# The rational feed-forward after a channel attention: the second product's input as two float32r parts, numerator and denominator as completed squares, in one arm of a branch

## The chip, the cores and the metric

One core of a Trainium2 chip. The metric is the device time of one execution in microseconds (us), the median of the runs; a smaller number is better. The engines are named as the profile names them: PE (TensorE, matrix products), ACT (ScalarE), DVE (VectorE), POOL (GpSimd) and SP (the queue that issues the DMAs here). SBUF is the on-chip memory, PSUM the banks that PE writes to.

## What is computed

```python
qn = q / (norm(q, axis=1) + 1e-6);  kn = k / (norm(k, axis=1) + 1e-6)   # q, k, v: 4 x 6080 x 256
s  = kn.transpose(0, 2, 1) @ qn / tau                                  # 256 x 256 per batch
a  = softmax(s)
x  = (v @ a).reshape(24320, 256)
h  = x @ w_in                                                          # 24320 x 2048
P  = a0 + a1*h + a2*h**2 + a3*h**3
Q  = 1 + |b0|*|h| + |b1|*h**2
out = (P / (Q + 1e-6)) @ w_out                                         # 24320 x 256
```

`w_in` and `w_out` are float64, all else is float32. The coefficients that the reference draws by default are a = (0.505, -0.235, -0.287, 0.280) and b = (-3.213, 3.898).

## The kernel before

The attention matrix is folded into the weights of the first layer: for each batch the kernel sums k'q over 24 half blocks of rows (`Attn.half`), makes the softmax (`Attn.softmax`) and multiplies it into `w_in` (`fuse`), which gives for each of 8 blocks of 256 hidden columns a high and a low float32r part (`whi`, `wlo`). After that the work is a long stream of pairs. There are 48 groups of tokens (12 per batch: 11 of 512 tokens and one of 448), and each group runs through 8 pairs (`pair`, line 620), a pair being 2 x 128 hidden columns by 512 tokens, 1024 elements on each of 128 partitions. So there are 384 pairs, worth 380 of full width.

A pair before has these steps (lines 633 to 696):

- `mm1` on PE: 12 float32r products (high x high, high x low, low x high) of 512 columns into `hx`, one of three PSUM slots.
- The denominator in `d`, in one of two forms. Five of eight pairs take the plain form: ACT squares `hx`, POOL makes b1*h^2 + 1 (`line`), ACT makes |b0*h| in `kk`, POOL adds the two (`sum`). The pairs in `FACTORED` (three of eight) take ACT, then DVE (`prod`), then ACT again.
- The numerator: ACT makes a3*h + a2 in `y`, DVE multiplies by h (`num1`), adds a1 and multiplies by h again (`num2`).
- The reciprocal: ACT takes the reciprocal root of `d` and squares it (`r`), POOL multiplies d*r (`again`; with `one` before it on factored pairs), DVE adds a0 and multiplies by r (`quot`), and DVE multiplies by 2 - d*r (`last`), a correction step, into `g`.
- `mm2` on PE: 4 float32 products of `g` with `w_out_sb`, each of which appears in the trace as two instructions of 512 columns, summed over the 8 pairs in `acc` (PSUM).

`values` loads v, transposes it on DVE and splits it in two (`vhi` on ACT, `vlo` on POOL) once per group, and `finish` transposes `acc` on DVE and stores it. While a batch runs, the next batch's 24 half blocks are squared on ACT, summed up on POOL (`ssq`) and multiplied on PE into an `hx` slot, which DVE adds to `sacc`.

At the start `piece` turns the float64 weights into float32 by integer steps on DVE (12 of the 16 pieces before the first pairs, in `EARLY`), beside the first batch's attention.

What sets the order: `Planner.order` (line 133) goes through all steps with a list of costs (the second argument of `step`) and priorities (`LAG`, `TIME`), picks for each engine the ready step of the lowest key whose buffers are free, and writes out one fixed order for each engine. `keep_in_program_order` holds each engine to it. A step marked `port`, and any step on POOL, isn't started by the planner beside another such step on the other of the two engines DVE and POOL.

Of the kernel before, what the change touches and what calls it, by code (L numbers as in the profile page):

```python
# [10 lines left out]
F32 = mybir.dt.float32  # L11
U32 = mybir.dt.uint32
F32R = mybir.dt.float32r
AF = mybir.ActivationFunctionType
# [6 lines left out]
LAG = {  # L21
    "first": (0.84, 4.52, 2.78, 3.73, 4.53, 2.33, 3.41, 3.6),
    "prod": (-11.23, -0.03, -11.23, 6.14, -11.23, -11.23, 5.27, -11.23),
    "abs": (-35.28, -33.04, -35.28, -60.18, -35.28, -35.28, -12.39, -35.28),
    "line": (-60.83, 30.85, 1.23, -9.96, -64.93, -61.3, 25.68, -3.97),
    "second": (3.47, 5.1, 5.85, 6.25, 8.47, 6.18, 3.15, 4.97),
    "sum": (-75.1, -80.53, -59.16, -66.42, -83.56, -73.41, -47.34, -36.63),
    "slope": (6.9, 4.95, 7, 7.41, 9.07, 6.95, 6.12, 6.22),
    "num1": (80.21, 21.96, 120.89, 23.72, 98.59, 65.28, 53.4, 94.99),
    "num2": (91.21, 77.02, 48.39, 83.69, 132.26, 79.9, 92.26, 66.3),  # L30
    "root": (-17.03, -9.24, -6.87, -5.73, -6.19, -9.62, -12.27, -14.71),
    "one": (18.62, -22.45, 18.62, 2.61, 18.62, 18.62, 25.53, 18.62),
    "square": (-78.86, -34.07, -129.08, -42.44, -147.95, -117.98, -7.49, -107.82),
    "again": (-10.9, -52.88, -8.31, -23.6, -7.9, 6.38, -36.31, -6.49),
    "quot": (38.4, 26.11, 35.76, 10.27, 43.7, 29.95, 4.71, 41.91),
    "last": (-3.36, 0.17, -3.01, -4.4, 0.77, 1.56, -1.89, -4.37),
    "out": (24.58, 54.15, 41.53, 45.99, 18.94, 61.33, 13.35, 15.28),
    "in": (-5.72, -5.59, -3.14, -6.52, -2.09, -4.66, -7.12, -10.04), "in_n": 0,
}
TIME = {  # L40
    "pair": 3.576, "start": 61.026, "load": 1.674, "softmax": 52.628, "in": 4.243, "late_in": 1.499,
    "out0": 30.295, "out": 5.035, "attn0_0": -1.487, "attn_0": 1.155, "attn0": 4.026, "attn": 1.97,
    "attn1": 91.474, "value": 54.159, "fuse": 1.698, "finish": 21.052, "front": 41.363,
    "front_pace": 1.762, "ahead": 15.518, "vhi": 26.968, "vlo": 25.086,
# [38 lines left out]
class Planner:  # L83
# [17 lines left out]
    def add(self, eng, cost, key, fn, reads=(), writes=(), port=False):  # L101
# [20 lines left out]
        for b in {id(b): b for b in (*reads, *writes)}.values():  # L122
            if b.tag is not None:
                b.left += 1
                s.bufs.append(b)
# [7 lines left out]
    def order(self):  # L133
# [19 lines left out]
        def fits(s):  # L153
            want = {}
            for b in s.new:
                want[b.tag] = want.get(b.tag, 0) + 1
                if b.tag in queue and queue[b.tag][-1] is not s:
                    return False
            if any(b.owner != s.eng and b.until > now for b in s.banks):
                return False  # L160
            return all(len(free[t]) >= n for t, n in want.items())
# [55 lines left out]
def tile_channel_attention_rational_ffn(  # L217
# [25 lines left out]
    while n0 < N:  # L243
# [7 lines left out]

    FACTORED = (1, 3, 6)

    EARLY = [("in", m) for m in range(8)] + [("out", m) for m in range(4)]

    FRONT = 12

# [6 lines left out]
    SLOTS = {"hx": 3, "acc": 1, "d": 4, "uu": 4, "r": 3, "g": 4, "w": 10, "kq": 4, "sq": 2, "ssq": 1,  # L264
             "vst": 1, "vhi": 2, "vlo": 2, "orow": 2, "sacc": 1, "eT": 1, "cv": 1, "cv2": 1, "n2": 1,
             "s0": 1, "y": 1, "e": 1, "sm": 1}
    plan = Planner(SLOTS, ("d", "uu", "r", "g", "w", "kq", "sq", "cv", "cv2", "vst", "vhi", "vlo", "orow", "acc"), ("hx", "acc"))

# [3 lines left out]

    homes = {}

    def buf(tag, shape, dtype=F32, name=None):


        def view(slot):
            sizes = dict(zip("abc", shape[1:]))
            t = homes[tag][slot]  # L280
            if t.dtype != dtype:
                t = t.bitcast(dtype)
            t = t[:, : math.prod(shape[1:])]
            names = " ".join(sizes)
            return t.rearrange(f"p ({names}) -> p {names}", **sizes) if len(sizes) > 1 else t

        homes.setdefault(tag, 0)
        homes[tag] = max(homes[tag], math.prod(shape[1:]))
        return Buf(tag, view)

    def step(eng, cost, key, fn, reads=(), writes=(), port=False):
        new = [b for b in writes if b.tag is not None and not b.writers]

        def run():
            for b in new:
                b.tile = b.view(b.slot)
            fn()

        plan.add(eng, cost, key, run, reads, writes, port)
# [6 lines left out]
    coef = const.tile([P, 7], F32, name="coef")  # L306
    sp.dma_start(coef[:, 0:4], ca.partition_broadcast(P))
    sp.dma_start(coef[:, 4:6], cb.partition_broadcast(P))
    sp.dma_start(coef[:, 6:7], tau.partition_broadcast(P))
    a0, a1, a2, a3 = (coef[:, i : i + 1] for i in range(4))  # L310
    rtau = const.tile([P, 1], F32, name="rtau")
    dve.reciprocal(rtau, coef[:, 6:7])

    babs = const.tile([P, 2], F32, name="babs")
    act.activation(babs, coef[:, 4:6], AF.Abs)
    b0, b1 = babs[:, 0:1], babs[:, 1:2]
# [458 lines left out]
```

## Time and profile before

| | |
|---|---|
| median of 3 runs | 2646.99 us (2646.87 to 2647.03) |
| span of the profiled execution (first to last instruction) | 2645.5 us |
| PE busy | 2595.5 us, 98% |
| DVE, POOL, ACT busy | 2259.8, 2216.3, 2124.2 us |
| chain that ended last | PE 88% |
| granted TensorE clock, mean | 0.995 of full speed |

The page gives no time of the profiled execution beside its span; the median of the other runs lies 1.5 us above it. "Busy" of PE is modelled from the starts of pipelined matmuls, so the chain and the distance between starts are read, not the mean of one instruction. In the timelines the start of one instruction is often ahead of the end of the one before on the same engine; what one costs in a full stream is the distance from its start to the next start.

### The profile page before, as it was taken

The numbers are of one execution on the slowest core, as the hardware profiler recorded it, in microseconds if no ns is written. First come the engines' busy times: TensorE is split into PE (matmuls) and PEld (weight loads), VectorE is DVE, ScalarE is ACT, GpSimd is POOL, SyncE is SP. The second block draws the span as 40 slices with busy tenths as digits, with TensorE's granted clock in tenths as the row PEclk, the third lists the DMA queues.
The fourth block names the chain that finished last, engine by engine and source line by source line (L and its number), as shares of the span: only waits on it lengthen the run. The fifth ranks groups of instructions, "written<-read, shape, count | busy, mean of one in ns | idle before, by whom it ended". The sixth has DMA issues, their size and how long they took to land.

```text
span 2645.5 us, 26474 instructions
## 1 busy us (share of the span) xinstructions
PE 2595.5 (98%) x8744; PEld 1651.8 (62%) x8744; DVE 2259.8 (85%) x2035; ACT 2124.2 (80%) x2179; POOL 2216.3 (84%) x1152
## 2 busy tenths in 40 slices
PE   7899999999999999999999999999999999999998
PEld 6656666666666666666666666665666566666665
DVE  6898888988978787888888878888897889889887
ACT  5688888888878778788878778778887888888886
POOL 6889888888778999788878899878885888888886
PEclk9899999999999999999999999999999999999999
DMA  9512311111112222211121222211111111111101
GB/s 306 153 25 64 68 19 25 23 17 24 17 35 53 48 65 53 48 24 17 23 40 16 49 68 51 46 25 17 23 25 17 18 22 24 22 18 25 23 9 15
DMA packets 457017, 109.76 MB, mean 41 GB/s; under 512 B 405168, under 2 KB 453808, under 8 KB 456880
## 3 DMA queue, kind: packets, MB, share of 16 engines
q1 hardware_dynamic: 456880, 108.07, 19.4%
q8 instruction: 69, 1.13, 0.2%
q14 instruction: 68, 0.56, 0.1%
HBM read 83.10 MB, written 24.90 MB: 41 GB/s over the span
## 4 chain that ended last, share of the span: by engine, by line
PE 88%; ACT 4%; DVE 3%; DMA 2%; issue 1%; POOL 1%; SPq 0%; DVEq 0%; ACTq 0%; POOLq 0%
PE acc L58 45%; PE hx L58 43%; ACT uu L58 1%; DVE hx L58 1%; DMA r<-in_k_dram 1%; ACT r L58 1%; ACT d L58 1%; POOL d L58 0%; DVE uu L58 0%; DMA r<-in_q_dram 0%; DMA kq<-in_k_dram 0%; SPq L58 0%; ACT sq L58 0%; DVE g L58 0%; POOL ssq L58 0%
## 5 line engine op out<-in xcount | busy, mean ns | idle before, releaser
L58 PE MATMUL acc<-g,w_out_sb 128*128 128x512 f32 (+1 forms) x3072 | 1349.7, 588 | 4.5 <-DVE orow L58 4.4
L58 POOL TENSOR_TENSOR d<-d,r 128x1024 f32<-128x1024 f32 (+1 forms) x384 | 906.5, 2364 | 166.9 <-ACT r L58 155.0
L58 PE MATMUL hx<-vhi,w 128*128 128x512 f32 (+1 forms) x3072 | 961.4, 420 | 7.4 <-DVE g L58 5.3
L58 PEld LDWEIGHTS acc<-g,w_out_sb 128*128 128x128 f32 x3072 | 581.2, 189 | 618.6 <-issue 592.4
L58 PEld LDWEIGHTS hx<-vhi,w 128*128 128x128 f32 x3072 | 578.2, 189 | 229.4 <-issue 94.3
L58 POOL TENSOR_TENSOR d<-d,uu 128x1024 f32<-128x1024 f32 (+1 forms) x243 | 575.6, 2369 | 35.0 <-ACT uu L58 20.5
L58 DVE TENSOR_TENSOR uu<-uu,hx 128x1024 f32<-128x1024 f32 (+1 forms) x384 | 462.4, 1204 | 149.9 <-ACT uu L58 148.8
L58 DVE SCALAR_TENSOR_TENSOR hx<-hx,coef,r 128x1024 f32<-128x1024 f32 (+1 forms) x384 | 489.2, 1275 | 111.3 <-ACT r L58 106.9
L58 ACT ACTIVATE d<-hx 128x1024 f32<-128x1024 f32 (+1 forms) x243 | 247.1, 1017 | 345.7 <-PE hx L58 338.6
L58 DVE SCALAR_TENSOR_TENSOR hx<-uu,coef,hx 128x1024 f32<-128x1024 f32 (+1 forms) x384 | 487.7, 1273 | 4.2
L58 DVE SCALAR_TENSOR_TENSOR g<-d,hx 128x1024 f32<-128x1024 f32 (+1 forms) x384 | 461.0, 1201 | 21.6 <-POOL d L58 15.0
L58 PE MATMUL hx<-vlo,w 128*128 128x512 f32 (+1 forms) x1536 | 473.7, 390 | 0.0
L58 ACT ACTIVATE uu<-hx,babs 128x1024 f32<-128x1024 f32 (+1 forms) x384 | 425.9, 1109 | 50.7 <-PE hx L58 50.7
L58 ACT ACTIVATE uu<-hx,coef 128x1024 f32<-128x1024 f32 (+1 forms) x384 | 461.4, 1201 | 1.3 <-DVE d L58 1.3
L58 ACT ACTIVATE r<-d 128x1024 f32<-128x1024 f32 (+1 forms) x384 | 405.4, 1056 | 20.2 <-POOL d L58 17.8
L58 ACT ACTIVATE r<-r 128x1024 f32<-128x1024 f32 (+1 forms) x384 | 405.2, 1055 | 6.8
L58 POOL TENSOR_SCALAR d<-d,babs 128x1024 f32<-128x1024 f32 (+1 forms) x243 | 272.2, 1120 | 133.8 <-ACT d L58 130.7
L58 PEld LDWEIGHTS hx<-vlo,w 128*128 128x128 f32 x1536 | 288.9, 188 | 60.7
L58 DVE SCALAR_TENSOR_TENSOR d<-uu,babs,hx 128x1024 f32<-128x1024 f32 (+1 forms) x141 | 178.2, 1264 | 33.7 <-ACT uu L58 33.4
L58 POOL TENSOR_SCALAR d<-d,ones 128x1024 f32<-128x1024 f32 (+1 forms) x141 | 157.5, 1117 | 36.7 <-ACT r L58 36.6
L58 POOL TENSOR_TENSOR ssq<-sq,ssq 128x1024 f32<-128x1024 f32 (+1 forms) x69 | 166.0, 2406 | 24.0 <-ACT sq L58 19.5
L58 ACT ACTIVATE d<-d 128x1024 f32<-128x1024 f32 (+1 forms) x141 | 146.8, 1041 | 9.8 <-DVE d L58 9.8
(82 smaller groups left out, 1119.1 us busy)
## 6 DMA issues: line engine op xcount, KB each, us to landing
vst<-in_v_dram SPq DMA_DIRECT2D x352, 64.0 KB, 2.3
out_dram<-orow SPq DMA_DIRECT2D x352, 64.0 KB, 2.0
kq<-in_k_dram SPq DMA_DIRECT2D x78, 256.0 KB, 3.8
kq<-in_q_dram SPq DMA_DIRECT2D x78, 256.0 KB, 4.2
d<-in_moe_w_in_dram SPq DMA_DIRECT2D x8, 512.0 KB, 7.0
r<-in_k_dram SPq DMA_DIRECT2D x10, 256.0 KB, 6.5
r<-in_q_dram SPq DMA_DIRECT2D x10, 256.0 KB, 6.5
d<-in_moe_w_out_dram SPq DMA_DIRECT2D x4, 512.0 KB, 8.2
```

The costliest lines, as they stand in the source:

```text
L58: ins = op(*args, **kwargs)
```

## The change

Steps of a pair, in the arm that runs when the tests on the coefficients hold:

- The hidden layer is scaled (by `grow`, put into the softmax's reciprocal) and the constants are transformed, so that the denominator is 1 + (|h| + centre)^2 and the numerator (h * ((reach*h + shift)^2 + drop) + a0'). ACT makes |h| and the square in `d`, the square in `y`; DVE makes `num` from `y` and `hx`. The plain and factored forms, `kk` and `num1` are gone in this arm.
- ACT makes the reciprocal root of d + 1 and squares it (`r`), as before.
- DVE makes gh = (num + a0') * r, rounded to float32r (`high`), then (d + 1) * gh (`back`, both inputs in SBUF, marked `port`), then num + a0' minus that (`rest`); POOL multiplies this remainder by r into gl (`low`, float32r).
- `w_out` is split in `piece` into `w_high` and `w_low` (float32r). `mm2` is 8 float32r products of gh with both, and 4 of gl with `w_high`.
- The test on the coefficients (4|a1||a3| >= a2^2, 3.5|b1| >= b0^2, and bounds) is computed on DVE at the start, loaded into a register of every engine, and a branch chooses between two complete programs, each with its own planned order. The loads of the first 7 half blocks stand ahead of the branch. The constants of the arm are made in `squares()` behind it.
- Slots: `uu` 3 (was 4), `w` and `w2` 9 (10), `orow` 1 (2), `g` becomes `gh` 3 and `gl` 2. The tables `LAG` and `TIME` are new, and so all the orders; `FACTORED` goes.

With the coefficients above, 4|a1||a3| = 0.264 against a2^2 = 0.082, and 3.5|b1| = 13.6 against b0^2 = 10.3.

```diff
 def pair(m, at, vparts, w, acc):
...
-        if m >= NFP and p in FACTORED:
...
-            step("POOL", 2.36 * s, at + LAG["sum"][p], fn, [d, kk], [d])
-        fn = lambda: act.activation(c(y), c(hx), AF.Identity, scale=a3, bias=a2)
-        fn = lambda: dve.tensor_tensor(c(y), c(y), c(hx), op=ALU.mult)
-        fn = lambda: dve.scalar_tensor_tensor(c(hx), c(y), a1, c(hx), op0=ALU.add, op1=ALU.mult)
+            if fast:
+                    on("ACT", 0.94, "size", lambda: act.activation(c(d), c(hx), AF.Abs), [hx], [d])
+                on("ACT", 1.06, "bow", lambda: act.activation(c(d), c(d), AF.Square, bias=centre), [d], [d])
+                fn = lambda: act.activation(c(y), c(hx), AF.Square, scale=reach, bias=shift)
+                on("ACT", 1.09, "slope", fn, [hx], [y])
+                fn = lambda: dve.scalar_tensor_tensor(c(hx), c(y), drop, c(hx), op0=ALU.add, op1=ALU.mult)
+                on("DVE", 1.2, "num", fn, [y, hx], [hx])
...
-        fn = lambda: pool.tensor_tensor(c(d), c(d), c(r), op=ALU.mult)
-        fn = lambda: dve.scalar_tensor_tensor(c(hx), c(hx), a0, c(r), op0=ALU.add, op1=ALU.mult)
-        fn = lambda: dve.scalar_tensor_tensor(
-            c(g), c(d), 2.0, c(hx), op0=ALU.subtract, op1=ALU.mult, reverse0=True
-        )
+            fn = lambda: dve.scalar_tensor_tensor(c(out), c(hx), base_a0, c(r), op0=ALU.add, op1=ALU.mult)
+            on("DVE", 1.2, "high", fn, [hx, r], [out])
...
+                fn = lambda: dve.scalar_tensor_tensor(c(d), c(d), 1.0, by(), op0=ALU.add, op1=ALU.mult)
+                on("DVE", 1.2, "back", fn, [d, near], [d], True)
...
+                fn = lambda: dve.scalar_tensor_tensor(c(into), c(hx), base_a0, c(d), op0=ALU.add, op1=ALU.subtract)
+                on("DVE", 1.2, "rest", fn, [hx, d], [into])
...
+                    on("POOL", 2.36, "low", lambda: pool.tensor_tensor(c(gl), c(d), c(r), op=ALU.mult), [d, r], [gl])
+                parts = ((1.82, "out_hi", gh, (w_high, w_low)), (0.91, "out_lo", gl, (w_high,)))
...
+    halves = {fast: arm(fast) for fast in (True, False)}
+    choice = nc.values_load(plain[0:1, 0:1], min_val=0, max_val=1)
+    with tc.If(choice > 0) as which:
+        squares()
+        for s in halves[True]:
+            s.fn()
+    with which.Else():
+        unscaled()
+        for s in halves[False]:
+            s.fn()
```

DVE in the middle of the stream, before. hx_90 to hx_92 are the three PSUM slots; uu<-uu,hx is `num1`, hx<-uu,coef,hx `num2`, hx<-hx,coef,r `quot`, d<-uu,babs,hx `prod`, and g is written by `last`:

```order
L58 SCALAR_TENSOR_TENSOR d_83<-uu_86,babs,hx_92 128x1024
L58 SCALAR_TENSOR_TENSOR hx_91<-uu_85,coef,hx_91 128x1024
L58 SCALAR_TENSOR_TENSOR hx_90<-hx_90,coef,r_108 128x1024
L58 SCALAR_TENSOR_TENSOR hx_91<-hx_91,coef,r_109 128x1024
L58 SCALAR_TENSOR_TENSOR g_96<-d_81,hx_90 128x1024
L58 TENSOR_TENSOR uu_87<-uu_87,hx_92 128x1024
```

Every one of these instructions has an operand in PSUM (hx).

DVE in the middle of the stream, now, in the arm that the coefficients choose. hx_68 to hx_70 are the PSUM slots, `fit` holds the constants; gh is written by `high`, hx<-uu,fit,hx is `num`, d<-d,gh `back`, d<-hx,fit,d `rest`:

```order
L56 SCALAR_TENSOR_TENSOR gh_82<-hx_70,fit,r_81 128x1024
L56 SCALAR_TENSOR_TENSOR hx_69<-uu_76,fit,hx_69 128x1024
L56 SCALAR_TENSOR_TENSOR d_75<-d_75,gh_82 128x1024
L56 SCALAR_TENSOR_TENSOR d_75<-hx_70,fit,d_75 128x1024
L56 SCALAR_TENSOR_TENSOR gh_83<-hx_69,fit,r_79 128x1024
L56 SCALAR_TENSOR_TENSOR hx_68<-uu_77,fit,hx_68 128x1024
L56 SCALAR_TENSOR_TENSOR d_73<-d_73,gh_83 128x1024
```

Four instructions make a pair; `back` has both inputs in SBUF, and `high` and `num` of later pairs stand between the `rest` of one pair and the `back` of the next. POOL's `low` becomes ready at `rest`.

PE where the first batch's fusing (hx<-w_in_sb) meets the first pair (hx<-vhi,w), before; acc<-kq is a half block of the next batch's scores:

```order
L58 MATMUL hx_92<-ident,sq_105 128x128 x4
L58 MATMUL hx_90<-w_in_sb,eT_115 128x256 x4
L58 MATMUL hx_91<-w_in_sb,eT_115 128x256 x4
L58 MATMUL hx_92<-w_in_sb,eT_115 128x256 x4
L58 MATMUL acc_89<-kq_102 128x256 x4
L58 MATMUL hx_90<-vhi_137,w_116 128x512 x2
```

Three of the eight blocks are fused ahead of the first pair, the others between the pairs that follow.

PE at the same place now (sq_100 holds the turned softmax, w_87 a part of the first fused block):

```order
L56 MATMUL hx_69<-kq_97 128x256 x4
L56 MATMUL hx_69<-kq_98 128x256 x4
L56 MATMUL hx_70<-ident,sq_101 128x128 x4
L56 MATMUL hx_68<-w_in_sb,sq_100 128x256 x4
L56 MATMUL hx_69<-w_in_sb,sq_100 128x256 x4
L56 MATMUL hx_70<-w_in_sb,sq_100 128x256 x4
L56 MATMUL hx_68<-w_in_sb,sq_100 128x256 x4
L56 MATMUL hx_69<-w_in_sb,sq_100 128x256 x4
L56 MATMUL hx_70<-w_in_sb,sq_100 128x256 x4
L56 MATMUL hx_68<-w_in_sb,sq_100 128x256 x4
L56 MATMUL hx_69<-w_in_sb,sq_100 128x256 x4
L56 MATMUL hx_70<-vhi_104,w_87 128x512 x2
```

All eight blocks are fused ahead of the first pair, and four more half blocks of the next batch's scores (two of them shown) stand ahead of it than before.

## Rows read from the trace of the kernel before

**Rows 1.** The page: span, and busy time of each engine.

```profile
span 2645.5 us, 26474 instructions
PE 2595.5 (98%) x8744; PEld 1651.8 (62%) x8744; DVE 2259.8 (85%) x2035; ACT 2124.2 (80%) x2179; POOL 2216.3 (84%) x1152
```

**Rows 2.** Chain that ended last, one group: start us, us, what, count.

```profile
2124.55 8.58 PE acc L58 x20
2133.13 5.49 PE hx L58 x24
...
2173.95 8.58 PE acc L58 x20
```

**Rows 3.** Windows: us, busy of PE, PEld, DVE, ACT, POOL, clock, DMA share, GB/s.

```profile
150.00:2600.00 2450.00, 2437.56 (x8163) 1536.05 (x8162) 2107.47 (x1853) 2006.55 (x2042) 2078.79 (x1083) 1.00 0.17 32
2124.00:2174.00 50.00, 50.00 (x164) 30.65 (x163) 43.76 (x37) 41.94 (x42) 42.13 (x23) 1.00 0.14 22
```

**Rows 4.** Groups of instructions: busy us, mean ns; idle before and releaser.

```profile
L58 POOL TENSOR_TENSOR d<-d,r 128x1024 f32<-128x1024 f32 x352 | 839.1, 2387 | 137.7 <-ACT r L58 126.5 <-DVE orow L58 1.2 <-DVE hx L58 0.6
L58 POOL TENSOR_SCALAR d<-d,babs 128x1024 f32<-128x1024 f32 x223 | 251.8, 1129 | 126.4 <-ACT d L58 123.3 <-DVE g L58 2.3
```

**Rows 5.** Timeline of DVE: start us, us, engine line op, names, shapes.

```profile
159.48 1.29 DVE L58 SCALAR_TENSOR_TENSOR hx<-hx,coef,r 128x1024 f32<-128x1024 f32 x1
160.67 1.28 DVE L58 SCALAR_TENSOR_TENSOR hx<-uu,coef,hx 128x1024 f32<-128x1024 f32 x1
161.86 1.22 DVE L58 SCALAR_TENSOR_TENSOR g<-d,hx 128x1024 f32<-128x1024 f32 x1
162.99 1.21 DVE L58 TENSOR_TENSOR uu<-uu,hx 128x1024 f32<-128x1024 f32 x1
```

**Rows 6.** Timeline of ACT in a stretch without waits.

```profile
2053.51 1.02 ACT L58 ACTIVATE d<-hx 128x1024 f32<-128x1024 f32 x1
2054.41 1.06 ACT L58 ACTIVATE d<-d 128x1024 f32<-128x1024 f32 x1
2055.36 1.21 ACT L58 ACTIVATE uu<-hx,coef 128x1024 f32<-128x1024 f32 x1
2056.45 1.06 ACT L58 ACTIVATE r<-d 128x1024 f32<-128x1024 f32 x1
2057.39 1.12 ACT L58 ACTIVATE uu<-hx,babs 128x1024 f32<-128x1024 f32 x1
2058.39 1.07 ACT L58 ACTIVATE r<-r 128x1024 f32<-128x1024 f32 x1
```

**Rows 7.** Timelines of DVE and POOL: DVE instructions with both inputs in SBUF.

```profile
15.09 1.23 DVE L58 TENSOR_TENSOR orow<-sq,orow 128x1024 f32<-128x1024 f32 x1 [0.74 <-POOL orow L58]
16.23 0.70 DVE L58 TENSOR_SCALAR acc<-d 128x512 uint32<-128x512 uint32 x1
...
70.11 0.43 DVE L58 SCALAR_TENSOR_TENSOR e<-e,s 128x258 f32<-128x258 f32 x1
70.58 2.56 DVE L58 SCALAR_TENSOR_TENSOR e<-y,e 128x258 f32<-128x258 f32 x1
...
70.50 2.35 POOL L58 TENSOR_TENSOR ssq<-sq,ssq 128x1024 f32<-128x1024 f32 x1 [8.34 <-ACT sq L58]
```

**Rows 8.** Timelines of DVE and PE at the start.

```profile
19.98 5.34 PE L58 MATMUL hx<-kq 128*128 128x256 f32 x24
...
9.94 0.69 DVE L58 TENSOR_SCALAR acc<-d 128x512 uint32<-128x512 uint32 x1 [5.13 <-DMA d<-in_moe_w_in_dram]
65.34 0.68 DVE L58 TENSOR_TENSOR orow<-orow 128x512 f32<-128x512 f32 x1
...
97.75 0.81 PE L58 MATMUL hx<-vhi,w 128*128 128x512 f32 x2
```

**Rows 9.** Windows of 3 us, columns as in Rows 3.

```profile
108.00:111.00 3.00, 0.21 (x1) 0.21 (x2) 3.00 (x5) 3.00 (x5) 3.00 (x3) 0.98 0.00 0
111.00:114.00 3.00, 3.00 (x8) 2.28 (x8) 3.00 (x3) 2.97 (x4) 3.00 (x2) 0.50 0.00 0
```

More of the change, by code (lines that the diff above doesn't have):

```diff
@@ L30 @@
[L30 to L36, printed above, removed]
@@ L99, in __init__, with add @@
         self.steps = []
-    def add(self, eng, cost, key, fn, reads=(), writes=(), port=False):
+    def add(self, eng, cost, key, fn, reads=(), writes=(), port=False, adds=()):
         s = Step()
@@ L158, in fits @@
                     return False
+            if s.port and port["POOL" if s.eng == "DVE" else "DVE"] > now:
+                return False
             if any(b.owner != s.eng and b.until > now for b in s.banks):
@@ L401, in tile_channel_attention_rational_ffn @@
[L401 to L426 removed]
+    whole = [p for p in range(NFP) if p in WHOLE]
@@ new lines, in tile_channel_attention_rational_ffn @@
+    split = [p for p in range(NFP) if p not in WHOLE]
+    at_w = {p: 2 * i for kind in (whole, split) for i, p in enumerate(kind)}
+    TERMS = 2 * len(whole) + 6 * len(split)
+    w_out_sb = const.tile([P, 2 * len(whole), C], F32, name="w_out_sb") if whole else None
+    w_high = const.tile([P, 2 * len(split), C], F32R, name="w_high")
+    w_low = const.tile([P, 2 * len(split), C], F32R, name="w_low")
+    fit = const.tile([P, 12], F32, name="fit")
+    sign, grow, centre, share, reach, shift, drop, zero, near, left, inv, base_a0 = (fit[:, i : i + 1] for i in range(12))
@@ new lines, in values @@
+            step("SP", 1.5, at - TIME["ahead"], load, gate, [vst])
+            whole = "p e i c -> p e (i c)"
+            fn = lambda: dve.transpose(vT[:, :, :n], vst[:, :, : n // 32].rearrange(whole))
+            step("DVE", 1.13, at, fn, [vst], [vT, hi, lo], True)
+            if VHI_ON_POOL and G:
+                fn = lambda: pool.tensor_scalar(hi[:, :, :n], vT[:, :, :n], 1.0, 0.0, op0=ALU.mult, op1=ALU.add)
+                step("POOL", 1.1, at + TIME["vhi"], fn, [vT], [hi])
+            else:
+                step("ACT", 0.95, at + TIME["vhi"], lambda: act.activation(hi[:, :, :n], vT[:, :, :n], AF.Copy), [vT], [hi])
@@ new lines, in finish, with store @@
+        def finish(G, at, acc):
+            b, g = divmod(G, NG)
+            base, pn = groups[g]
+            n = T * pn
+            orow = buf("orow", [P, NC2, GT // 32, 32])
+            fn = lambda: dve.transpose(orow[:, :, : n // 32].rearrange("p e i c -> p e (i c)"), acc[:, :, :n])
+            step("DVE", 1.2, at, fn, [acc], [orow])
+            row = b * N + base
+            def store():
+                to = out[row : row + n].rearrange("(i t) (e j c) -> j e t i c", t=32, e=NC2, c=32)
+                for j in range(4):
+                    for e in range(NC2):
+                        sp.dma_start(to[j, e], orow[32 * j : 32 * j + 32, e, : n // 32])
+            step("SP", 1.5, at + 2, store, [orow], [Buf()])
@@ new lines, in arm @@
+        for n, (side, m) in enumerate(EARLY):
+            c = 8.0 + TIME["in"] * n
+            piece(side, m, min(c, 36.0 + 0.1 * n) - 6.0 if side == "in" else c - 6.0, c)
+        late = [("out", m, TIME["out0"] + TIME["out"] * m) for m in range(NFP) if ("out", m) not in EARLY]
+        for n, (side, m, c) in enumerate(sorted(late, key=lambda x: x[2])):
+            piece(side, m, T0 + c - 12.0, T0 + c)
+        attns = [Attn(0, 0.0, TIME["load"], TIME["softmax"])]
+        vparts = [values(0, TIME["softmax"])]
```

849 lines of the change are left out of this document (469 added, 380 removed).

## The prediction

> **What bounds the kernel now.** I read the page first, then the chain, then windows, then timelines. The page has PE busy for 98% of a span of 2645.5 us, DVE for 85%, POOL 84%, ACT 80% [rows 1]. PE's busy time is modelled, so the chain has to confirm it: over a whole group without work for the next batch, from 2124.55 to 2173.95, the chain is PE alone, products into `acc` and into `hx` in turn [rows 2]. 49.40 us for 8 pairs is 6.18 us a pair. From 150 to 2600 us PE idles 12 of 2450 us [rows 3]. So the stream runs at PE's pace. In the same window of 50 us DVE is busy 43.8, POOL 42.1, ACT 41.9 [rows 3]: all three are within 17% of being the bound, so how much of a cut on PE is kept depends on what they need afterwards.
>
> **PE, the gain.** In the chain 20 instructions of the old `mm2` take 8.58 us, 0.429 each, and 24 float32r instructions of `mm1` take 5.49, 0.229 each, both at 512 columns [rows 2]. A pair has 8 of the first and 12 of the second: 3.43 + 2.75 = 6.18, which is the group's pace. The new `mm2` is 12 float32r products: 2.75. The pair becomes 5.49, the group 43.9 instead of 49.4. The gain is 0.69 us a pair, times 380 full pairs: **262 us**, if PE stays the bound.
>
> **ACT.** Before: five instructions a pair. After: five again. Distances between starts give the price [rows 6]: |h| from PSUM as d<-hx, 0.90; the square with a per-partition bias between 0.95 (d<-d, no such operand) and 1.05 (0.10 more, the difference of uu<-hx,babs to d<-hx); y as uu<-hx,coef, 1.09; the root 0.94; its square 0.95 as d<-d. Together 4.83 to 4.93; I take the upper, since a per-partition operand is there. Eight pairs and one `vhi` make some 40.4 us of a group's 43.9. ACT isn't the bound, with 8% to spare.
>
> **POOL.** It loses most: `line` 1.13, `sum` and `again` 2.39 each [rows 4] become one `low` of 2.39. With `vlo` a group needs 21.5 of 43.9 us.
>
> **DVE.** A pair needs `num` (as hx<-uu,coef,hx, 1.19), `high` (as hx<-hx,coef,r, 1.19, or 1.13 if writing SBUF makes it like g<-d,hx), `rest` (1.13 to 1.19) [rows 5], and `back` with both inputs in SBUF, 1.14 from its start to the next by the nearest row [rows 7]. I take 4.65 a pair, 37.2 a group, and two transposes at about 1.2: **39.6 us** of 43.9. That leaves 0.53 us a pair for waits.
>
> **The wait that the change adds.** `back` and POOL's instructions read SBUF through something that they share. At 70.58 DVE's e<-y,e took 2.56 us, while its like just before took 0.43; POOL's instruction ran from 70.50 to 72.85, and DVE ended 0.29 after it [rows 7]. So a `back` that comes while `low` runs waits for the rest of `low`, anything from 0 to 2.39 us, and behind it on DVE stand `rest`, the next `high` and `num`, for which PE's next product and the `hx` slots wait. By the new order `high` and `num` (2.38 us) stand between a `rest` and the next `back`, and `low` (2.39) becomes ready at that `rest`. The two fit almost exactly; what sticks out is the hand-over, and I take 0.2 us a pair, 1.6 a group. A `vlo`, or an `ssq` while the next batch is summed, comes between: two POOL instructions of 2.39 in a row reach some 1.3 us beyond the next `back` (4.8 less `rest` and two more of DVE, 3.5). One `vlo` a group makes DVE 42.5 of PE's 43.9. In a group that also takes four half blocks of scores, DVE gets 4 x 1.3 of wait and two additions of about 0.7: 49.1. PE gets 32 instructions at 0.22 [rows 8], 7.1 us: 51.0. PE stays the later one in both, but only by 3 or 4%, and the order is fixed, so uneven waits cost. PE's idle time in the stream is 0.5% now [rows 3]; I add 12 us to it (0 to 70, the upper being DVE as the bound by 1.5 us a group).
>
> The Trainium skill (SBUF — State Buffer, § SBUF: two separate sides) says that a DVE instruction with two SBUF inputs and a GpSimd instruction that reads SBUF exclude each other for the whole instruction, whoever starts first. That speaks against `back`, and the trace agrees, with 2.56 us against 0.43.
>
> **The start.** Before, the first conversion on DVE starts at 9.94, the squares' sum is folded at 65.34, and the first pair's product starts at 97.75 [rows 8]. Now the weights' loads stand behind the branch, and DVE makes the test and then the constants, some 50 dependent instructions of one column; from nothing to 0.47 each (the distance of the two rows at 70 us, on 258 columns [rows 7]), 0 to 23 us; I take 0.2, so 10. The fold stands behind all 12 early pieces instead of 9, and `w_low` is one instruction more a piece. Against this the softmax afterwards has no pieces in between, all eight blocks are fused when the first pair starts, and four half blocks of later work are done (7 us). I take **+10** for the start, 0 to 30.
>
> For the branch itself only a page has a price. The Trainium skill (Advanced Engine Details and Errata, § Control Flow Timing) gives about 0.11 us for a compare-and-branch, by which the sum would move by 0.1 us; it adds (Runtime: NRT & Kernel Launch, § Instruction fetch mechanics) that a taken branch to code that isn't loaded waits for its fetch, which no run here shows.
>
> The end, one pair's way through the engines and a store, is about as long as before: 0.
>
> **Sum.** The median lies 1.5 us above the span, and I keep that. 2647 - 262 + 12 + 10 = **2407 us**.
>
> **Rivals.** 1. *The shared path makes DVE the bound, and most of the gain stays.* If a `back` waits 0.85 us on average (a third of a `low`) instead of 0.2 plus the extra instructions, a group takes 39.6 + 6.8 = 46.4 us on DVE, 2.5 more than PE needs, over 47.5 full groups 119 us: about 2515. For it: the margin is 3%, and ACT and PE set when `low` starts as much as the order does. Against: where DVE and POOL alternate, one waits at most once a pair.
>
> 2. *The same wait eats everything, and the kernel is slower.* The point is (49.4 - 39.6)/8 = 1.23 us a `back`, half a `low`. At a full `low` of wait, 2.39, the group takes 58.7 us: 2647 + 47.5 x 9.3 + 10 = 3100. For it: POOL has nothing else to do and starts `low` the moment `rest` ends; if `high` or `num` comes late, `back` comes late too, but if they came before `rest` then `back` stands right behind it and waits a full `low`. Against: in the rows of the order shown two instructions stand between.
>
> 3. *The general arm runs.* It has POOL's 1.13 + 2.39 + 2.39 and a `back` in the way, 7.05 us a pair, 58.8 a group with `vlo`, again about 3100. Against: the test holds by factors of 3.2 and 1.3 for these coefficients. This is also the case that the change doesn't do what it says.
>
> 4. *TensorE's clock.* In the 3 us from 108, PE was nearly idle, and in the next 3 the granted clock was 0.50, the lower level of 1.2 GHz [rows 9]. New gaps of that length would cost twice: 1.5 us of lost work for each such window. One a group would make 72 us: about 2480. The waits above are shorter than that gap, so I count it with rival 1.
>
> **Chances.** Forecast 0.78, between 2365 (faster starts than 0.2 us of the small instructions, no added waits, and 7 us done early; the term of PE at 0.225 instead of 0.229) and 2450 (the upper of either unknown). Rivals 1 and 4 together 0.13 (2450 to 2620). Within 0.2%: 0.02. Rivals 2 and 3: 0.07. A measurement of this kernel can tell some 0.2% from no change. Faster 0.91, same 0.02, slower 0.07. The range that should hold 8 in 10 takes the forecast's and the nearer part of rival 1: 2365 to 2500.
>
> **What would show it.** In the chain of the new profile a group in the stream should take 43.9 us, PE alone, with `acc` and `hx` both at 0.229 an instruction; if `acc` is slower the first term falls. `back` (d<-d,gh) should have a mean near 1.4 us; near 2 or more is rival 1 or 2, and then DVE is the engine that PE's waits name. ACT's five should sum to 4.9. POOL's `low` should stay at 2.39, and POOL be half idle. The first pair's product should start between 100 and 130 us. A clock below 1 in the stream would be rival 4.

## The result, and the profile after

The changed kernel takes 2461.6 us (median of 4 runs, 2459.0 to 2462.2) against 2646.9 before: a ratio of 0.930, interval 0.9285 to 0.9311, or 185 us less. The forecast was 2407, so 240 us less: the side and the range hold, and 55 us of the gain are missing. The profiled execution took 2459.0 us for a span of 2457.2.

The page after, to be read against [rows 1]:

```profile
span 2457.2 us, 29203 instructions
PE 2370.8 (96%) x10280; PEld 1939.5 (79%) x10280; DVE 2177.2 (89%) x1953; ACT 2156.1 (88%) x2187; POOL 1330.9 (54%) x525
```

PE has 224.7 us less work and DVE only 82.6, ACT has 32 more, POOL lost 885. So the three engines that share the stream are now within 9% of each other on the page.

The chain that ended last, one group between two products of 20 instructions (start us, us, what, count), answers to [rows 2]:

```profile
2123.97 4.59 PE acc L56 x20
2128.57 2.79 PE hx L56 x12
2131.36 1.85 PE acc L56 x8
...
2168.37 4.59 PE acc L56 x20
```

This chain reaches back only to 1887 us, 23% of the span; in the clean part of the stream, a stretch without work for a next batch, it is PE alone. A group takes 44.40 us (2168.37 less 2123.97) instead of 49.40: 5.00 us a group, 237 us over 47.5 groups.

Windows (us, busy of PE, PEld, DVE, ACT, POOL, clock, DMA share, GB/s), first the three stages, then one clean stretch, then the stretch in which the second batch takes over:

```profile
0.00:150.00 150.00, 113.68 (x462) 92.84 (x462) 115.65 (x201) 86.14 (x108) 81.49 (x40) 0.90 0.68 210
150.00:2412.00 2262.00, 2225.19 (x9667) 1818.42 (x9668) 2031.49 (x1728) 2046.09 (x2054) 1231.72 (x478) 0.99 0.17 34
2412.00:2458.00 46.00, 31.98 (x152) 28.28 (x151) 30.09 (x26) 23.87 (x26) 17.65 (x8) 0.86 0.14 24
2100.00:2150.00 50.00, 50.00 (x218) 40.57 (x217) 46.67 (x39) 47.42 (x47) 25.98 (x11) 1.00 0.13 22
650.00:700.00 50.00, 43.78 (x207) 38.68 (x205) 43.62 (x53) 37.12 (x48) 22.80 (x10) 0.97 0.08 14
700.00:750.00 50.00, 48.72 (x212) 39.22 (x212) 38.66 (x39) 45.55 (x51) 21.31 (x9) 1.00 0.11 18
750.00:800.00 50.00, 48.09 (x210) 39.02 (x209) 43.33 (x37) 43.81 (x45) 31.63 (x13) 1.00 0.28 65
```

PE idles 36.3 us in the first 150 (29.9 before, by a window of the same bounds), 36.8 in the stream (12.4 before [rows 3]) and 14.0 in the last 46 (8.2 before). In the clean stretch it idles not at all, but DVE has 46.7 and ACT 47.4 of 50, against 43.8 and 41.9 before [rows 3]. Most of the stream's loss sits at the three changes of batch, 27.1 us, of which the first is shown: PE idles 9.4 us there (6.2, 1.3 and 1.9 in the three windows); before, the first change, at 700 to 800, cost 2.4, and all three 7.3. Another 7.3 us are idle in the first 100 us of this stage.

What ends PE's waits there (timeline of PE; in brackets the idle time ahead and what ended it):

```profile
657.87 0.68 PE L56 MATMUL acc<-gh,w_high 128*128 128x448 f32 x2 [1.34 <-DVE orow L56]
685.91 0.33 PE L56 MATMUL hx<-ident,sq 128*128 128x128 f32 x1 [3.48 <-ACT sq L56]
688.13 1.11 PE L56 MATMUL acc<-gh,w_high 128*128 128x448 f32 x2 [1.17 <-DVE gh L56]
```

PE stands in the softmax's row of dependent steps (`sq` are its exponentials), then waits for a `gh` that DVE made late, and after that gap its instructions are slower for a while: 1.11 us for two of 448 columns, against 0.68 at 657.87, which also stands behind a wait. In the 2 us from 688 the granted clock is 0.50, the lower level of 1.2 GHz (columns as above):

```profile
688.00:690.00 2.00, 1.87 (x5) 1.70 (x6) 2.00 (x3) 0.62 (x1) 1.30 (x1) 0.50 0.00 0
```

Over the whole stream (150 to 2412) the two largest of PE's waits are these (what it waited for: us in total, times, longest):

```profile
PE hx L56 <- DVE d L56: 19.6, 16, 2.5
PE hx L56 <- ACT sq L56: 10.6, 4, 3.5
```

The first is a product into `hx` that waits until `rest` (which writes `d`) has read the slot: half of the stream's 36.8 us.

The groups of the new steps (busy us, mean ns; idle before and releaser), full width only:

```profile
L56 POOL TENSOR_TENSOR gl<-d,r 128x1024 fp32r<-128x1024 f32 x352 | 884.7, 2517 | 891.5 <-DVE d L56 494.8 <-ACT d L56 229.9 <-PE acc L56 147.6
L56 DVE SCALAR_TENSOR_TENSOR d<-d,gh 128x1024 f32<-128x1024 f32 x352 | 485.2, 1379 | 2.5
L56 DVE SCALAR_TENSOR_TENSOR d<-hx,fit,d 128x1024 f32<-128x1024 f32 x352 | 448.8, 1276 | 6.5
L56 POOL TENSOR_TENSOR vlo<-cv,vhi 128x1024 fp32r<-128x1024 f32 x44 | 136.8, 3110 | 18.5 <-ACT vhi L56 18.5
```

`back` (d<-d,gh) has a mean of 1379 ns where 1.4 us was forecast, 0.10 above `rest` (d<-hx,fit,d), which has one input in PSUM. POOL pays for its part of the path to SBUF that it shares with DVE: `low` 2517 (the forecast took 2387 [rows 4]), and `vlo` 3110 (2386 before).

The start, to be read against [rows 8] (timelines of DVE and PE):

```profile
6.28 0.16 DVE L56 RECIPROCAL fit<-size 128x1 f32<-128x1 f32 x1 [0.68 <-DVE rtau L56]
12.13 2.70 DVE L56 TENSOR_TENSOR fit<-fit 128x1 f32<-128x1 f32 x4
14.94 2.32 DVE L56 TENSOR_TENSOR fit<-fit 128x1 f32<-128x1 f32 x1
17.92 0.70 DVE L56 TENSOR_SCALAR acc<-d 128x512 uint32<-128x512 uint32 x1 [0.67 <-DMA d<-in_moe_w_in_dram]
82.44 2.60 DVE L56 TENSOR_TENSOR orow<-orow 128x512 f32<-128x512 f32 x1
...
122.67 0.82 PE L56 MATMUL hx<-vhi,w 128*128 128x512 f32 x2
139.21 1.22 PE L56 MATMUL acc<-gh,w_high 128*128 128x512 f32 x2 [7.81 <-DVE gh L56]
```

The constants run from 6.28 to 17.3, the first conversion starts 8 us later than before, the fold 17, the first pair 25. PE's longest waits in this stage, beside the one at its very start, are 8.07 us for a load of `q` (until 74.77), 7.40 for the softmax's exponentials (until 105.04) and 7.81 for the first `gh`.

### The profile page after: what moved, and what is told of

It is laid out like the page before. It is cut to its first block, busy times and chain, and to the rows that moved or that the text cites. A ratio compares the mean times of both kernels' runs of the same rounds, so it can differ in the third digit from the quotient of the medians.

```text
span 2457.2 us, 29203 instructions
## 1 busy us (share of the span) xinstructions
PE 2370.8 (96%) x10280; PEld 1939.5 (79%) x10280; DVE 2177.2 (89%) x1953; ACT 2156.1 (88%) x2187; POOL 1330.9 (54%) x525
## 5 line engine op out<-in xcount | busy, mean ns | idle before, releaser
L56 POOL TENSOR_TENSOR gl<-d,r 128x1024 fp32r<-128x1024 f32 (+1 forms) x384 | 957.1, 2496 | 989.2 <-DVE d L56 561.7
L56 DVE SCALAR_TENSOR_TENSOR hx<-uu,fit,hx 128x1024 f32<-128x1024 f32 (+1 forms) x384 | 488.0, 1271 | 89.0 <-ACT uu L56 88.7
L56 DVE SCALAR_TENSOR_TENSOR gh<-hx,fit,r 128x1024 fp32r<-128x1024 f32 (+1 forms) x384 | 485.1, 1263 | 76.3 <-ACT r L56 73.1
L56 DVE SCALAR_TENSOR_TENSOR d<-d,gh 128x1024 f32<-128x1024 f32 (+1 forms) x384 | 525.9, 1370 | 2.6
L56 PE MATMUL acc<-gh,w_high 128*128 128x512 f32 (+1 forms) x1536 | 482.8, 396 | 14.7 <-DVE gh L56 10.6
L56 DVE SCALAR_TENSOR_TENSOR d<-hx,fit,d 128x1024 f32<-128x1024 f32 (+1 forms) x384 | 485.3, 1264 | 6.7
L56 PE MATMUL acc<-gh,w_low 128*128 128x512 f32 (+1 forms) x1536 | 476.1, 391 | 0.0
L56 ACT ACTIVATE uu<-hx,fit 128x1024 f32<-128x1024 f32 (+1 forms) x384 | 457.4, 1191 | 0.0
L56 ACT ACTIVATE d<-d,fit 128x1024 f32<-128x1024 f32 (+1 forms) x384 | 437.4, 1140 | 0.0
L56 PE MATMUL acc<-gl,w_high 128*128 128x512 f32 (+1 forms) x1536 | 407.8, 392 | 2.9 <-POOL gl L56 2.9
L56 POOL TENSOR_TENSOR vlo<-cv,vhi 128x1024 fp32r<-128x1024 f32 (+1 forms) x48 | 149.4, 3112 | 18.5 <-ACT vhi L56 18.5
```

Of the source, the lines that this page charges most:

```text
L56: ins = op(*args, **kwargs)
```

## The experiments

Each is one edit of the changed kernel, if nothing else is said, run beside the kernel before on the same chip (2647.0 to 2647.5 us). Where no range stands beside a time, it is one run. In the code "..." stands for lines left out. "The order" is the sequence of steps on each engine, which the planner writes out from step lengths and priorities.

**The chosen arm without the branch.**

```diff
...
-    choice = nc.values_load(plain[0:1, 0:1], min_val=0, max_val=1)
-    with tc.If(choice > 0) as which:
-        squares()
-        for s in halves[True]:
-            s.fn()
...
+    squares()
+    for s in arm(True):
+        s.fn()
```

> The chosen arm alone, without the register load, the branch and the other arm; orders, loads and constants as in the changed kernel (2461.6 us). Theory A, that the branch costs next to nothing because the register is loaded within 0.7 us after the test and the first seven loads are on their way: within 5 us of 2461.6. Theory B, that the branch and the code behind it are a main part of the missing gain of some 54 us: 2440 or less.

Measured: 2457.5 us (2456.6 to 2458.6), ratio 0.9283 (0.9267 to 0.9298). The medians differ by 4.2 us, so the branch, with the load of the register and the second copy of the program, costs some 4 us, as theory A has it; the two intervals overlap, so the size is rough.

**The second product in float32 again, all else new.**

```diff
...
-                acc[:, e, :n], w[:, at_w[p] + i, e * P : (e + 1) * P], x[:, i, :n],
+                acc[:, e, :n], w[:, at_w[p] + i, e * P : (e + 1) * P].bitcast(F32), x[:, i, :n].bitcast(F32),
...
-                fn = lambda x=x, ws=ws: mm2(x, ws)
+                fn = (lambda: None) if name == "out_lo" else lambda x=x: mm2(x, (w_high,))
```

> All orders and all steps on ACT, DVE and POOL as in the changed kernel, but the second product is again 4 float32 products (8 instructions) of gh with w_high, and the products with w_low and of gl are left out (the output lacks them). Theory A, that PE's second product is the whole gain: a group at 49.3 to 49.6 us, total 2670 to 2700. Theory B, that the shorter elementwise chain gives a good part of it: total below 2620.

Measured: 2757.2 us, 110 slower than the kernel before, so both expectations were too low. Four products, which are eight instructions of 0.429, and 12 of 0.229 are what the kernel before had in a pair, and where PE is busy throughout, `acc` has the old pace (8 instructions in 3.43 us). But PE isn't busy throughout (a line of the page, then one of the chain; the span is 2755.4 us):

```profile
PE 2636.0 (96%) x8744; PEld 1656.1 (60%) x8744; DVE 2208.2 (80%) x1953; ACT 2160.8 (78%) x2187; POOL 1307.4 (47%) x525
2153.16 3.43 PE acc L56 x8
```

PE idles 119 us, against 50 before, and is busy for 41 us more. The order was kept, and it was written for products of another length; that this is what lets PE wait is likely but not shown, as no order was planned for the float32 product with all else new. Two things follow. In this order the cheaper products carry the whole gain: without them the other parts of the change bring nothing. And the time lies some 60 us beyond the upper end of A, so an experiment that changes an instruction's length and keeps the order can measure the order as well.

**POOL's `low` without the second input** (the product with `r` is left out, so the low part of the quotient is another number).

```diff
-                    on("POOL", 2.36, "low", lambda: pool.tensor_tensor(c(gl), c(d), c(r), op=ALU.mult), [d, r], [gl])
+                    on("POOL", 2.36, "low", lambda: pool.tensor_scalar(c(gl), c(d), ones[:, 0:1], 0.0, op0=ALU.mult, op1=ALU.add), [d, r], [gl])
```

> POOL's product low (2.4 to 2.5 us) becomes a one-input instruction of about 1.1 us that leaves out the factor r (the output lacks it); every order stays. Theory A, that the path shared by DVE and POOL costs nothing in the stream because PE is the bound: the group stays at 44.4 us, the total within 10 us of 2461.6, while back's mean falls from 1.38 to about 1.22. Theory B, that the waits behind low set the pace: a group at 43.9 or less and a total of 2435 or less.

Measured: 2461.1 us (2460.1 to 2462.3), the same as the changed kernel. The two groups (columns as above):

```profile
L56 DVE SCALAR_TENSOR_TENSOR d<-d,gh 128x1024 f32<-128x1024 f32 (+1 forms) x384 | 482.0, 1256 | 2.6
L56 POOL TENSOR_SCALAR gl<-d,ones 128x1024 fp32r<-128x1024 f32 (+1 forms) x384 | 468.3, 1221 | 1377.9 <-DVE d L56 737.9 <-PE acc L56 490.0 <-issue 105.8
```

`back`'s mean falls from 1370 (both widths) to 1256 and `low` from 2496 to 1221, so `back`'s wait on the shared path is gone, 44 us of DVE's time in all, and the end doesn't move, as theory A has it. The Trainium skill (SBUF — State Buffer, § SBUF: two separate sides) has the two engines exclude each other when DVE's instruction has two SBUF inputs and GpSimd's reads SBUF; the trace agrees (2.60 us for the fold at 82.44, 0.68 before), and this run adds that it costs the total nothing while PE is the bound.

**The low part's products left out** (4 of a pair's 12 second products; the order and all other steps stay).

```diff
...
-                fn = lambda x=x, ws=ws: mm2(x, ws)
+                fn = (lambda: None) if name == "out_lo" else lambda x=x, ws=ws: mm2(x, ws)
```

> PE leaves out the 4 products of gl (0.92 us a pair, 7.4 a group); every order and every step on the other engines stays. PE would need 37.0 us a group. Theory A, that DVE and ACT are 5 to 8% behind PE as the next bounds: a group at 41 to 42.5 us and a total of 2330 to 2380. Theory B, that DVE with its waits already sets the 44.4: total above 2430.

Measured: 2433.5 us, 28 less, where PE had 4 x 0.23 = 0.92 us less to do in each of 380 pairs, 350 us. A group (chain, from one first product to the same one of the next group) takes 44.12 us, 0.28 less than with the products:

```profile
2098.22 3.07 PE hx L56 x12
2101.31 1.03 ACT d L56
...
2141.10 1.20 DVE d L56
2142.34 3.07 PE hx L56 x12
```

and its window:

```profile
2150.00:2200.00 50.00, 44.66 (x187) 34.06 (x186) 48.96 (x40) 47.67 (x48) 26.81 (x11) 1.00 0.18 30
```

Now the chain goes from PE to ACT, to DVE and back to PE, and DVE is busy for 98%, ACT 95%: theory B. So in this order the loop of ACT and DVE stands right behind PE, 0.3 us a group away. In the changed kernel's stream PE and this loop are within 1% of each other, so what is taken off PE alone hardly shows. The order is again one that was written for more work on PE; whether another would let the loop turn faster wasn't run. And part of DVE's 98% is the shared path: `back` of full width has a mean of 1491 ns here, against 1266 beside the light `low`, some 1.8 us a group. What costs nothing while PE is the bound counts once it isn't.

**No change of batch, after and before.** All groups use the first batch's fused weights; the softmaxes and fusings of batches 2 to 4 are left out. The same two edits in both kernels:

```diff
-                self.softmax(end)
+                if first:
+                    self.softmax(end)
...
-                pair(G * NFP + p, at + p * II, vparts[G], attns[b].w[p], acc)
+                pair(G * NFP + p, at + p * II, vparts[G], attns[0].w[p], acc)
```

> The changed kernel without the softmax and the fusing of batches 2 to 4: all batches use the first one's weights (so three quarters of the output are not the reference's); their scores and sums of squares are still made. PE's work in one switch is about 15.6 us (8 fused blocks of 1.73, norms, turns). Theory A, that each switch costs PE about 9 us of idle time and 3 us of lower clock on top of that: total 75 to 95 us below 2461.6. Theory B, that the switches cost their work alone: 45 to 50 us below.

> The same cut in the kernel before (2646.9 us). Its trace shows about 2.4 us of idle PE in a switch: total 50 to 58 us below 2646.9 by theory A of the run before, and about as much as in the changed kernel by theory B.

Measured: 2405.5 us after (56 less, 18.7 a change of batch), 2628.5 before (18.5 less, 6.2 a change). Neither expectation was met, and the pair doesn't say what it was meant to say. The planner made a new order for each. After, PE's busy time falls by 53.1 us (2317.7 of a span of 2403.6) and its idle time stays at 86: the windows from 650 to 800 lose 3.3 us instead of 9.4, others lose more. Without the softmaxes the waits in the stream are many short ones for `d` (22 of them, 22.8 us) and for `orow` (9, 11.9 us). Before, the span falls by 18.8 us and PE's busy time by 32.2, so less is won than PE's left-out work. So the cost of a change of batch can't be read from leaving it out, since the idle time follows the order. This stays inconclusive for the place; for the sum it says that 86 us of idle PE are what these priorities give here, with the softmaxes or without.

**The general arm alone** (for rival 3; no branch).

```diff
...
-        for s in halves[True]:
-            s.fn()
...
+    unscaled()
+    for s in arm(False):
+        s.fn()
```

> The other arm alone, without the branch: the quotient as two parts and the new second product, but the denominator and numerator in the general forms. Theory A (the prediction's price): POOL needs 1.13 + 2.39 + 2.39 a pair and waits for back, 1.14, on the shared path: 58.8 us a group, about 3100. Theory B, that PE's shorter product is enough for a gain with either form: below 2640.

Measured: 3286.9 us. Its groups for `back` and POOL's `line`:

```profile
L56 DVE SCALAR_TENSOR_TENSOR d<-d,gh 128x1024 f32<-128x1024 f32 (+1 forms) x384 | 673.1, 1754 | 7.8 <-DVE gh L56 0.9
L56 POOL TENSOR_SCALAR d<-d,size 128x1024 f32<-128x1024 f32 (+1 forms) x384 | 523.4, 1363 | 338.7 <-ACT d L56 319.5
```

It is POOL's and the shared path's case: `back` is 0.5 us longer than beside the light `low`, `line` takes 1363 instead of 1129 [rows 4]. So rival 3 had the right mechanism and a price 190 us too low, as it took POOL at the lengths of before and its idle time (338.7 us ahead of `line`) at nothing. It isn't what ran: the changed kernel has no kk and no `line` in its trace.

**The constants later.** They are issued ahead of the first conversion of `w_out` instead of `w_in`, where DVE waits 4.43 us for a transfer.

```diff
...
             def low_bits():
+                if side == "out" and fits:
+                    fits.pop()()
...
-        squares()
+        fits.append(squares)
```

> The arm's one-column constants stand, on every engine, right ahead of the first conversion of the output weights instead of ahead of the first conversion of the input weights; everything else keeps its order. In the changed kernel they hold VectorE from 6.28 to 17.3 us, of which 5.0 us are two instructions that wait for GpSimd, and the first conversion starts at 17.92. At the new place VectorE waits 4.43 us for the output weights' transfer anyway (until 63.13). Theory A: the way to the first pair runs through VectorE from the start (conversions, the sums of squares, the fold at 82.44), so the first conversion starts near 10 and the first pair comes some 5 to 8 us earlier: 2453 to 2457. Rival B: the way to the first pair is held by the loads of the first batch (TensorE waited 8.07 us for one of them at 74.77), and the constants cost nothing there: 2460 to 2463, the fold still past 80.

Measured: 2469.3 us (2467.3 to 2469.8), 7.7 slower than the changed kernel; neither expected that. Two rows of DVE's timeline, then the issue of the first load of `w_in` in the changed kernel and in the one before:

```profile
19.13 0.69 DVE L56 TENSOR_SCALAR acc<-d 128x512 uint32<-128x512 uint32 x1 [13.54 <-DMA d<-in_moe_w_in_dram]
92.97 1.61 DVE L56 TENSOR_TENSOR orow<-orow 128x512 f32<-128x512 f32 x1
12.03 1.29 SPq L56 DMA_DIRECT2D d<-in_moe_w_in_dram  x3
4.15 0.47 SPq L58 DMA_DIRECT2D d<-in_moe_w_in_dram  x1
```

With nothing to do, DVE waits 13.54 us for the first `w_in` and starts at 19.13, no earlier than with the constants ahead. The weights' loads stand behind the 14 transfers of `k` and `q` that are begun ahead of the branch, so the first is issued at 12.03 instead of 4.15, and the constants lie in that wait. At the new place they hold DVE for 14 us, of which 4.4 are covered: the fold comes 10.5 us later and the end 7.7. So at their place in the changed kernel the constants cost nothing, as rival B has it, and a fold that comes this much later moves the end by three quarters of that. In the changed kernel itself the fold is not what PE waits for: it ends at 85.04, and PE comes to the product that needs it at 87.82, from other products and without a wait.

**The planner's lengths, and its priorities.** PE's steps get the lengths of the trace, once with the priorities of the changed kernel, once with priorities searched anew and DVE's first 8 us set aside for the constants.

```diff
-            on("PE", 2.73, "in", mm1, [whi, wlo, vhi, vlo], [hx])
+            on("PE", 2.78, "in", mm1, [whi, wlo, vhi, vlo], [hx])
...
-                parts = ((1.82, "out_hi", gh, (w_high, w_low)), (0.91, "out_lo", gl, (w_high,)))
+                parts = ((1.84, "out_hi", gh, (w_high, w_low)), (0.92, "out_lo", gl, (w_high,)))
```

> The changed kernel with one edit: the planner is told TensorE's lengths as measured (1 to 2% longer), the priorities stay. This shows how much the order hangs on small differences. Theory A: a plan nearer to the chip gives an order at least as good: 2450 to 2462. Rival B: the priorities are fitted to the lengths that were written there, and another order by the same priorities loses more at the changes of batch than the better lengths give: 2463 to 2485.

> The same work as the changed kernel in another order: the planner is given the lengths of TensorE's steps as the trace of the changed kernel has them (2.78, 1.84 and 0.92 us instead of 2.73, 1.82 and 0.91) and VectorE's constants at the start, and its priorities are searched anew with these. Theory A: the changed kernel loses some 9 us of TensorE's time at each of three changes of batch, and 8 at the end, because steps that VectorE and ScalarE owe TensorE come late in a fixed order; an order that fits the lengths gets back a third to a half of that: 2440 to 2455. Rival B: these losses are the work that VectorE and ScalarE have there, in any order: 2456 to 2470.

Measured: 2471.6 us (2471.1 to 2473.3) with the old priorities, 10 slower, as rival B has it; 2457.2 us (2453.9 to 2458.6) with new ones, 4 faster, which is in rival B's range and 2 us above theory A's. So a change of 1 to 2% in the lengths that the planner is told moves the end by 10 us through the order alone, with the same instructions.

**A new order.** As the last run, with the search for priorities carried on (the tables of numbers `LAG` and `TIME`; the instructions are the same).

> The same instructions as the changed kernel, with the planner's lengths of TensorE's steps as measured and its priorities searched much further than in the run before. Theory A: the 86 us in which TensorE idles in the changed kernel, 50 in the kernel before, are mostly the order's and not the work's; half of what it loses in the stream and at the start comes back: 2420 to 2445, with the group in the clean stretch still near 44.4. Rival B: the losses at the changes of batch are the softmax's dependent steps, which no order hides, and the better plan doesn't carry over to the chip: 2450 to 2465.

Measured: 2442.6 us (2441.7 to 2444.2), ratio 0.9226 (0.9210 to 0.9241): 19 us faster than the changed kernel, and the fastest of all that compute the whole. A group in the clean stretch is the same (44.38 us between two products of 20). The first two stages, and the first change of batch (windows as above); then one wait of PE in the stream, and a row of its timeline in that change:

```profile
0.00:150.00 150.00, 113.19 (x462) 92.70 (x462) 114.28 (x200) 83.69 (x106) 75.48 (x38) 0.91 0.64 203
150.00:2396.00 2246.00, 2219.55 (x9660) 1818.58 (x9661) 2037.03 (x1728) 2050.15 (x2056) 1232.59 (x479) 0.99 0.18 35
650.00:700.00 50.00, 49.05 (x238) 43.61 (x237) 44.60 (x52) 37.43 (x46) 23.91 (x11) 1.00 0.13 33
700.00:750.00 50.00, 46.99 (x208) 40.10 (x207) 27.98 (x35) 38.65 (x47) 39.05 (x17) 0.97 0.50 136
750.00:800.00 50.00, 49.12 (x217) 40.62 (x217) 37.35 (x31) 39.85 (x41) 36.13 (x15) 1.00 0.45 124
PE hx L51 <- ACT sq L51: 3.5, 1, 3.5
702.11 3.62 PE L51 MATMUL hx<-kq 128*128 128x256 f32 x16
```

In the stream PE idles 26.4 us instead of 36.8. At the three changes it idles 4.8, 3.9 and 7.6 us, 16.4 together, instead of 27.1. Over the whole execution its busy time is 4.7 us less for the same instructions, which fits fewer of them running behind a gap. The first 150 us lose what they lost (36.8). So the total is theory A's, and 40% of the loss at the changes of batch was the order's. The rows show how: PE's wait for the softmax's exponentials, four times in the changed kernel, comes once. At the first two changes the new order has PE make products of the next batch's scores (hx<-kq) there; at the third there is no next batch, and most of the loss stays, as rival B would have it. For the start theory A does not hold.

## Why the prediction was right, and where it missed

**The number: inside the range, beyond the forecast's own band.** 2461.6 us lies in 2365 to 2500, the range for 8 in 10. It lies above 2450, where the forecast's band (0.78) ended and that of rivals 1 and 4 (0.13) began; rival 1 did not happen, and rival 4's clock makes only a part of the difference. The band's ends don't follow from its terms: 70 us of waits instead of 12 give 2465, not 2450, and the terms named for the lower end some 2360, not 2365.

**That PE is the bound, and that the product sets the gain: right.** In the clean stream the chain is PE alone, a group is 5.00 us shorter, and with the float32 product put back, in the same order, the kernel is slower than before.

**The term of 262 us: mis-sized, 237.** It took 24 products a pair at 0.229. The group of 192 takes 44.40, so 0.231 each. The rows show where: `acc` keeps 0.229 to 0.231 (20 in 4.59, 8 in 1.85), `mm1` takes 2.79 for its 12, 0.04 more than forecast. `mm1` wasn't changed, and a block of 12 took 2.75 in the stream of the kernel before, where it stood alone as it does now:

```profile
2209.97 2.75 PE hx L58 x12
```

In the run with the float32 product the block takes 2.79 as well, so the new products beside it are not the reason. Why it costs 0.04 more stays open. 0.06 us a pair, with `acc`'s share, is 24 us of the missing 55, the largest single part.

**The margin of DVE and ACT: too wide.** The forecast gave ACT 40.4 us of 43.9, 8% to spare, and DVE 39.6, or 42.5 with its waits on the shared path, 3% to spare. In the clean stretch they are busy for 42.1 and 41.4 of 44.40 (95 and 93%), and with less on PE the two, in this order, go no faster than 44.1. For ACT the rows show what distances in a stretch without waits leave out (timeline of ACT):

```profile
2127.47 1.15 ACT L56 ACTIVATE d<-d,fit 128x1024 f32<-128x1024 f32 x1
2128.51 1.05 ACT L56 ACTIVATE vhi<-cv 128x1024 fp32r<-128x1024 f32 x1
2133.50 1.15 ACT L56 ACTIVATE d<-d,fit 128x1024 f32<-128x1024 f32 x1
2134.74 1.06 ACT L56 ACTIVATE r<-d 128x1024 f32<-128x1024 f32 x1
```

From the square in `d` to `vhi`, which doesn't need it, are 1.04 us, and to the root of that same `d` 1.24, where the forecast took 1.05. For DVE the busy time is near the forecast; what the forecast left out is the time in which DVE and ACT wait for each other and for PE within one turn. So a slack of 3 to 8% was, in this order, one of less than 1%. In the clean stretches this cost nothing, as PE is still the later one. At the changes of batch, where DVE and ACT have the softmax on top, PE waits for them; that a wider margin would have taken this up is argued, as no run widened it.

**The stream's waits, +12 (0 to 70): in the range, low.** PE's idle time rose by 24 us, from 12.4 to 36.8, and the changes of batch with some 7 us more each make 20 of it. The cause that the forecast named was the wrong one: the shared path makes `back` 0.1 us longer (0.2 was forecast) and costs the end nothing when taken away. The cause in its place is in part the order: 10 us of idle time and 5 of busy time came back with another order of the same instructions. What is left at the changes, 16 us, no run took away.

**The start, +10 (0 to 30): the size near, the reason wrong.** PE idles 6.4 us more in the first 150, and the granted clock is 0.90 there instead of 0.93 (a window of before with the same bounds). The constants took 11.0 us where 10 were forecast (5.0 of them in two rows that waited for POOL), but they lie in a wait for the first weights' load, which the transfers begun ahead of the branch hold up. What moved the fold by 17 us is what stands ahead of it: the first conversion starts 8 us later for the load, and three more early pieces and three `w_low` stand between it and the fold; and the fold itself waited 1.9 us for POOL. But PE waited elsewhere, for `q`, for the exponentials and for the first `gh`. All eight blocks are fused before the first pair (15.85 us at 107.17), which is work done early and not lost; but PE then waits 7.81 us for the first `gh`, where the kernel before had blocks left to fuse between its first pairs and waited 3.76 at most.

**The end, 0: low.** PE idles 14.0 instead of 8.2 us in the last 46, at a clock of 0.86 instead of 0.94. PE's timeline shows where:

```profile
2445.26 1.68 PE L56 MATMUL acc<-gl,w_high 128*128 128x448 f32 x4 [2.92 <-POOL gl L56]
```

Before, PE worked without a gap to its last product. Now the last pair's `back`, `rest` and `low` stand one behind the other in the chain (from 2439.63 to 2445.21), and the last products wait 2.9 us for that `gl`. From PE's end to the end of the execution it takes 10.3 us instead of 7.6, and why that grew was not looked into by a run.

**The sum again, by the trace.** PE's products -237, PE's idle time +6 (start), +24 (stream), +6 (end): -201. The span fell by 188. The 13 between them are busy time: it fell by 225 and not by 237. That fits products at the lower clock behind the gaps, at the start, at the changes of batch and at the end, where the clock reads 0.86 to 0.97; how much each place makes wasn't measured. The forecast had the clock as a rival with one gap a group; it came as a small term at the places of the gaps.

**The branch, nothing: right within 4 us.** The Trainium skill (Advanced Engine Details and Errata, § Control Flow Timing) has 0.11 us for a compare-and-branch; the trace has 0.84 us from DVE's last instruction ahead of the branch to the first constant (5.44 to 6.28), which includes the load of the register, and 0.07 where the branch is left out.

**The rivals.** The shared path (1 and 2) fell with the run without it. The general arm (3) didn't run, and would have taken 3287 us, not 3100. The clock (4) fell behind single gaps and not once a group. The float32 product with this order ends on the other side, slower by 110; the forecast knew that the order is fixed, but had no rival in which the order itself is the price.

## What to carry to other kernels

When a change takes work off the bound, sum the next engines with the hand-overs between them, over one turn of the loop, and not from distances in a stretch without waits: two engines that look 3 to 8% off can be the bound's equals. Where the order is fixed in advance, it is fitted to the lengths of the steps; after a change of lengths the order is a term of the sum in its own right (here -19 to +10 us by priorities and lengths alone), largest where extra work meets a full loop. And before you cost a step on the way to the start, look at what the step behind it waits for: 11 us of constants were free because a load was late.

## What the runs showed of the hardware

- The shared path catches the smallest instructions too: four DVE instructions of one column, 0.15 us each elsewhere, took 2.70 us together and a single one 2.32 while POOL worked (12.13 and 14.94 in the start's rows).
- It also lengthens POOL's side: `vlo` took 3110 ns on average, the same instruction 2386 before, and `low` 2517, the same kind of product 2387 before.
- On ACT a step that needs the result of the one just before it starts 0.20 us later than one that doesn't (1.24 against 1.04 us from start to start, at 2133.50 and 2127.47).
- Where PE comes out of a wait, its first two products take 0.56 us to the next start, 0.46 in the full stream, at a granted clock of 1.00 in both (2098.22 in the run without the low part's products, 2128.41 in the changed kernel). The 3.07 us of that block in the chain, against 2.79, hold this 0.10; the rest is the modelled end of the last product, which in a full stream the next start cuts off.
